# Four small fp32 transposing matmuls, moved along the TensorE queue from the first second product to the third quarter of the first w1

## Chip, cores and metric

The kernel runs on one core of a Trainium2 chip. The metric is the device time of one execution in microseconds, as a median of several runs; before the change it is 359.48 us (three runs, 359.46 to 359.53).

## What is computed

Attention over 4 batches and 8 heads, 768 tokens of 64 numbers, in which a token sees the 128 last tokens and 4 sink tokens; and behind it a mixture of four expert networks over the 3072 tokens, each token's experts weighted with its normalised probabilities.

```python
keep = is_sink | in_window                      # 4 sinks, window of 128
a = softmax(where(keep, q @ k.T / sqrt(D), -1e9))
x = (a @ v)                                     # heads side by side: [3072, 512]
p = domain_probs / (domain_probs.sum(-1, keepdims=True) + 1e-09)
for e in range(4):
    h = maximum(x @ w1[e], 0.0)                 # 512 -> 1024
    out += p[:, e:e + 1] * (h @ w2[e])          # 1024 -> 512
```

## The kernel before

**Tiling and stages.** Tokens are taken in groups of 256 (three groups g a batch b). For each group attention gives a transposed tile `xT` of bf16. For each expert e a *first product* makes H = relu(x w1): it is worked in four quarters j of 256 hidden columns, each 8 matmuls into one PSUM bank `hps` (L1114), after which ACT (L1127) or DVE (L1129) writes the quarter of H to SBUF. A *second product* multiplies H by w2 in 8 matmuls into one of two PSUM banks `acc[0]` and `acc[1]` (L1453), used in turn; ACT (L1465) or DVE (L1469 to L1471) then scales by the token's probability and adds to the output tile. Later groups take a form with seven products in place of eight for both (L1202, L1376); the change doesn't touch them.

**Who sets the order.** The program is written out by a planner in Python: the loop at the end of the kernel holds a clock for each engine (`t`), for each bank the time when it is free (`ring`, `acc_free`), and a list of tasks that other engines still have to run; at each turn it emits the candidate that is ready first. Every engine then works its own list strictly in the order in which the planner emitted it, and waits for semaphores where its data come from elsewhere. What matters here of the planner: `acc_free[i]` tells it when bank `acc[i]` may be written again, and a bank that counts as free may also be given to idle matmuls that it puts in where PE would stand still.

**The stretch of the change.** It lies in the first batch, some 18 to 24 us into the span. In the order of PE's list:

- the first product of the first group with expert 0: quarters 0 and 1 (L1114), with score matmuls (L738) and sink scores (L699) between them, then score matmuls, then quarter 2, the third
- the value products of attention (L798 and L805), which DVE normalises (reciprocal L832, product L835 into `onat`), and the transposes of the result (L864), which are copied to `xT` by DVE or ACT
- quarter 3 of expert 0 and four more transposes (L864)
- the four matmuls of `gates` (L966), and the first second product (L1453), into `acc[0]`

`gates` (L963 to L974) turns the probabilities: they are loaded as `dp`, 24 rows (blocks of 128 tokens) of 128 x 4 numbers, by one DMA of SP's queue (L478), issued right after the first q rows and ahead of the sinks (L546). One matmul for each expert, with a 24 x 24 fp32 identity, turns 24 x 128 into 128 x 24 in `acc[1]`. DVE sums over the experts (L968), adds a small number (L969), takes the reciprocal (L970) and multiplies (L971) into `scale_t`, which the scaling of all second products of the first batch reads. DVE also normalises the same probabilities by row for the later batches (L484 to L487); the two lists of instructions lie among each other on DVE.

w1 of expert 0 comes in four quarters by four DMAs of POOL's queue (L353), its w2 in two halves (L364), all issued early and landing one after the other; the first matmul of a quarter waits for that quarter's landing. `acc[1]` holds nothing else before its first second product: only the warming and idle matmuls of zeros (L533) write to it.

Of the kernel before, what the change touches and what calls it, by code (L numbers as in the profile page):

```python
# [16 lines left out]
def kernel(  # L17
# [17 lines left out]
    E, Dm, F = moe_w1.shape  # L35
# [71 lines left out]
    t = {"pe": 1200.0, "act": 0.0, "dve": 0.0, "pool": 1280.0, "sp": 800.0, "sw": 5900.0, "hw": 0.0}  # L107
    def by(x):

        return x[sum(t["pe"] > at for at in SPLIT)]  # L110
# [5 lines left out]
    def pe(cols, *deps, n=1, switch=0):  # L116
        t["pe"] = max([t["pe"], *deps])
        rate = 2.4 if t["pe"] > WARM else 1.2
        t["pe"] += cols / rate + 2.5 * n + 95 * switch
        return t["pe"] + 215  # L120
# [6 lines left out]
    def dve(cols, *deps, rate=0.96, fixed=157):  # L127
        at = max([t["dve"], *deps])
        t["dve"] = at + fixed - 85 + cols / rate
        return at + fixed + 35 + cols / rate  # L130
# [10 lines left out]
    def pick(part=True):  # L141

        return min(range(6), key=lambda i: (max(ring[i], t["pe"]), part == whole[i], ring[i]))

    def bank(i, shape, dtype, name, all_columns=False):

        whole[i] = all_columns
        return psum.tile(shape, dtype, name=name, tag=f"r{i}", bufs=1)

    def take(i, until):  # L150
        ring[i] = until
# [3 lines left out]
    def later(engine, ready, slack, run):  # L155

        pend.append((ready, ready + slack, engine, run))
# [35 lines left out]
    def clock(engine, cols, rate=0.96, fixed=157):  # L193
        return act(cols) if engine == "act" else dve(cols, rate=rate, fixed=fixed)
# [175 lines left out]
    def halves(e):  # L370
        return [slice(0, Dout)] if e else [slice(0, Dout // 2), slice(Dout // 2, Dout)]
# [99 lines left out]
    NT = Ntok // P  # L471
# [35 lines left out]
    def load_gates():  # L507

        while gates_at[0] < 1e11 and len(gate_sb) < len(mix.order) and (
            len(gate_sb) < NGATE or mix.order[len(gate_sb) - NGATE] in mix.finished  # L510
        ):
            b, g, e = mix.order[len(gate_sb)]
            load_gate(b * NG + g, e)
# [14 lines left out]
    acc = [psum.tile([P, 2 * G], FP32, name=f"acc{i}", tag=f"o{i}", bufs=1) for i in range(2)]  # L528
# [431 lines left out]

    scale_t = consts.tile([P, NT, E], FP32, name="scale_t")

    def gates():  # L963
        pt = acc[1][:, 0:E * NT].rearrange("p (e t) -> p e t", e=E)
        for e in range(E):
            nc.tensor.transpose(pt[:, e], dp[:, :, e], identf[0:NT, 0:NT])  # L966
        rs = consts.tile([P, NT], FP32, name="rs")
        nc.vector.reduce_sum(out=rs, in_=pt.rearrange("p e t -> p t e"), axis=AX.X)  # L968
        nc.vector.tensor_scalar_add(out=rs, in0=rs, scalar1=1e-9)  # L969
        nc.vector.reciprocal(out=rs, in_=rs)  # L970
        nc.vector.tensor_mul(  # L971
            scale_t, pt.rearrange("p e t -> p t e"), rs[:, :, None].to_broadcast([P, NT, E]),
        )
        acc_free[1] = dve(600, pe(400, acc_free[1]))  # L974

    PAIRS = [(b, g) for b in range(1, B) for g in range(NG)]
    CHAIN = ("P1", "P2", "P6", "P5", "P7", "P3", "P4")
    acc_free = [0.0, 0.0]
    out_sb = {}

    class Mixture:
# [96 lines left out]
        def emit_first(self, what, ready):  # L1078

            if what[0] == "early":  # L1080
                g = what[1]
                e = self.early[g].pop(0)
                u = self.opened(0, g, e)
                self.open.append(u)
                j = u["left"][0]
            elif what[0] == "unit":
                if not gate_sb:
                    load_gates()
                u = self.opened(*self.units.pop(0))
                self.open.append(u)  # L1090
                j = u["left"][0]
            else:
                u, j = what
            b, g, e = u["unit"]
            if j in (0, "P1") and (b, e) == (0, E - 1) and not gate_sb:
                load_gates()
            u["left"].remove(j)
            if not u["left"]:
                self.open.remove(u)
                left1[e] -= 1  # L1100
                if (b, g) not in PAIRS:
                    self.second += [(g, s, e, c) for c in halves(e) for s in range(2)]
            self.since += 1
            self.credit += (2 * QF * P if u["fast"] else 2 * NDB * G)
            if u["fast"]:
                self.emit_fast(u, j, ready)
                return
            slot = pick(False)
            h = bank(slot, [P, 2, G], FP32, "hps", True)
            ring[slot] = 1e12  # L1110
            for i in range(2):
                fb = 2 * j + i
                for db in range(NDB):
                    nc.tensor.matmul(  # L1114
                        h[:, i].rearrange("p (q n) -> p q n", q=2), lhsT=w1_sb[e][:, db, fb * P:(fb + 1) * P],
                        rhs=xT[b, g][:, :, db],
                        start=(i == 0 and db == 0), stop=(db == NDB - 1), skip_group_check=True,
                    )
            end = pe(2 * NDB * G, ready, n=2 * NDB)
            self.done += 2 * NDB * G  # L1120
            dst = self.H[b, g, e][:, j // 2, 2 * (j % 2):2 * (j % 2) + 2]
            dst = dst.rearrange("p f t n -> p f (t n)")
            part = self.H_part[b, g, e]
            if (b, g) not in PAIRS:
                def run(engine):
                    if engine == "act":
                        nc.scalar.activation(out=dst, in_=h, func=AF.Relu)  # L1127
                    else:
                        nc.vector.tensor_scalar(out=dst, in0=h, scalar1=0.0, scalar2=None, op0=ALU.max)  # L1129
                    at = clock(engine, 2 * G)  # L1130
                    take(slot, at)
                    part(at)
                later("any", end, 400, run)
                return
            gate = gate_sb[b * NG + g, e].rearrange("p t n -> p (t n)")[:, None, :].to_broadcast([P, 2, G])

            def run(engine):
                nc.vector.scalar_tensor_tensor(
                    out=dst, in0=h, scalar=0.0, in1=gate, op0=ALU.max, op1=ALU.mult,
                )  # L1140
                at = dve(2 * G, fixed=152)
                take(slot, at)
                part(at)
            later("dve", end, by(GATE0), run)
# [290 lines left out]
        def emit_second(self):  # L1435
# [5 lines left out]
            if g not in out_sb:  # L1441
                out_sb[g] = mo.tile([P, 2, Dout], FP32, name="osb0", tag=f"wide{g}" if g < 2 else "osb", bufs=1)
                if g == 0:
                    gates()
                    ready = max(ready, acc_free[self.turn % 2])
# [77 lines left out]
    while mix.more() or att.more():  # L1523
# [49 lines left out]
        s2, p = mix.second_ready(), mix.product_ready()  # L1573
# [67 lines left out]
```

## Time and profile before

| What | Value |
|---|---|
| median of the runs | 359.48 us (359.46 to 359.53) |
| the profiled execution: its time | 359.52 us |
| its span, first to last instruction | 357.8 us |
| granted TensorE clock | 1.000 |
| DVE, ACT, POOL busy | 296.2, 172.1, 69.0 us |
| the four matmuls L966 | first start 22.85 us, busy 0.65 us |

All durations in the text come from that one profiled execution, so they stand against its 359.52 us; the 1.7 us beside its span lie before the first and after the last instruction. A line such as `22.85 0.65 PE L966 MATMUL acc<-scratch 24*128 24x24 f32 x4` of the timeline is: start in us, length in us from the first start to the last end, engine, line of the kernel, operation, tiles written and read, shapes, how many; a bracket behind it tells how long the engine stood idle before it, and what ended that. PEld is the loading of weights, which overlaps with PE's matmuls. In the chain of waits a row is start, length, engine and line.

### The profile page before, as it was taken

The numbers are of one execution on the slowest core, as the hardware profiler recorded it, in microseconds if no ns is written. First come the engines' busy times: TensorE is split into PE (matmuls) and PEld (weight loads), VectorE is DVE, ScalarE is ACT, GpSimd is POOL, SyncE is SP. The second block draws the span as 40 slices with busy tenths as digits, with TensorE's granted clock in tenths as the row PEclk, the third lists the DMA queues.
The fourth block names the chain that finished last, engine by engine and source line by source line (L and its number), as shares of the span: only waits on it lengthen the run. The fifth ranks groups of instructions, "written<-read, shape, count | busy, mean of one in ns | idle before, by whom it ended". The sixth has DMA issues, their size and how long they took to land.

```text
span 357.8 us, 10767 instructions
## 1 busy us (share of the span) xinstructions
PE 350.9 (98%) x4525; PEld 302.6 (85%) x4534; DVE 296.2 (83%) x635; ACT 172.1 (48%) x440; POOL 69.0 (19%) x89
## 2 busy tenths in 40 slices
PE   8999999999999999999999999999999999999996
PEld 4688859757768698898998899899999999999985
DVE  5896689856978799899789889789899997898750
ACT  5958717458964555557455565554223203313110
POOL 8844117220942191010200000000000000000000
PEclk9999999999999999999999999999999999999999
DMA  9999999999999999168990211213111112000021
GB/s 174 185 190 204 210 207 176 184 156 179 131 144 169 191 146 165 49 63 151 141 124 22 54 44 50 60 62 60 31 45 62 31 31 76 16 29 33 0 75 45
DMA packets 115261, 37.26 MB, mean 104 GB/s; under 512 B 96533, under 2 KB 110709, under 8 KB 115213
## 3 DMA queue, kind: packets, MB, share of 16 engines
q0 software_dynamic: 75456, 17.31, 52.6%
q1 hardware_dynamic: 38700, 18.75, 26.2%
q8 instruction: 35, 0.57, 0.7%
q10 hardware_dynamic: 1056, 0.52, 0.6%
q14 instruction: 14, 0.11, 0.1%
HBM read 40.45 MB, written 9.49 MB: 140 GB/s over the span
## 4 chain that ended last, share of the span: by engine, by line
PE 94%; DVE 2%; DMA 2%; ACT 1%; issue 0%; ACTq 0%
PE cps L1202 34%; PE acc L1376 31%; PE acc L1453 12%; PE hps L1114 8%; PE sps L738 3%; PE od L805 3%; DMA raw<-in_k_dram 2%; DVE aT L773 1%; PE od L798 1%; DVE onat L835 1%; PE tx L864 0%; ACT aT L764 0%; PE sinks L699 0%; DVE H L1129 0%; PE tr L632 0%
## 5 line engine op out<-in xcount | busy, mean ns | idle before, releaser
L1202 PEld LDWEIGHTS <-w 128*128 128x128 bf16 x1248 | 76.8, 98 | 2.5 <-issue 0.6
L1376 PEld LDWEIGHTS <-H 128*128 128x128 bf16 x600 | 55.1, 98 | 7.3 <-issue 2.0
L764 ACT ACTIVATE aT<-sps 128x512 bf16<-128x512 f32 (+1 forms) x96 | 47.1, 575 | 24.6 <-PE sps L738 24.3
L1235 DVE SCALAR_TENSOR_TENSOR H<-cps,gates 128x512 bf16<-128x512 f32 x84 | 56.4, 681 | 1.5 <-PE cps L1202 0.7
L1376 PE MATMUL acc<-w,H 128*128 128x256 bf16 x360 | 49.4, 273 | 0.0
L1202 PEld LDWEIGHTS <-vf 128*128 128x128 bf16 x768 | 47.2, 98 | 1.6 <-issue 0.3
L1202 PE MATMUL cps<-T,w 128*128 128x128 bf16 x624 | 47.3, 219 | 0.0
L1202 PE MATMUL cps<-xT,w 128*128 128x128 bf16 x624 | 46.6, 219 | 0.0
L1453 PE MATMUL acc<-w,H 128*128 128x512 bf16 (+1 forms) x231 | 45.2, 335 | 0.5
L844 ACT ACTIVATE onat<-od,R 128x64 bf16<-128x64 f32 x144 | 33.0, 331 | 23.3 <-DVE R L832 23.2
L1248 ACT COPY cps<-cps 128x512 f32<-128x512 f32 x39 | 22.8, 584 | 41.8 <-PE cps L1202 35.2
L1202 PE MATMUL cps<-T,vf 128*128 128x128 bf16 x512 | 38.1, 219 | 0.0
L1114 PE MATMUL hps<-xT,w 128*128 128x256 bf16 x288 | 36.0, 273 | 0.9 <-DMA w<-in_moe_w_dram 0.9
L1453 PEld LDWEIGHTS <-H 128*128 128x128 bf16 x240 | 22.5, 98 | 14.3 <-issue 0.3
L340 POOL DMA_DIRECT2D vx<-in_v_dram x24 | 21.3, 895 | 59.9 <-PE od L805 47.4
L1114 PEld LDWEIGHTS <-w 128*128 128x128 bf16 x288 | 27.1, 98 | 5.1 <-DMA w<-in_moe_w_dram 1.5
L1376 PEld LDWEIGHTS <-S 128*128 128x128 bf16 x288 | 27.4, 98 | 3.3 <-issue 0.4
L1255 DVE TENSOR_TENSOR cps<-H,cps 128x512 f32<-128x512 f32 x33 | 22.8, 691 | 8.0 <-PE cps L1202 5.7
L1418 ACT COPY osb<-acc 128x256 f32<-128x256 f32 x28 | 10.5, 376 | 33.3 <-PE acc L1376 33.2
L1270 DVE TENSOR_TENSOR H<-H,cps 128x512 f32<-128x512 f32 x33 | 22.5, 682 | 3.9 <-PE cps L1202 3.8
L1261 ACT COPY H<-cps 128x512 f32<-128x512 f32 x33 | 19.7, 596 | 9.5 <-PE cps L1202 9.5
L1376 PE MATMUL acc<-wf,H 128*128 128x256 bf16 x176 | 23.7, 273 | 0.0
(130 smaller groups left out, 550.8 us busy)
## 6 DMA issues: line engine op xcount, KB each, us to landing
w<-in_moe_w_dram POOLq DMA_DIRECT2D x6, 1024.0 KB, 20.9
out_dram<-osb SPq DMA_DIRECT2D x19, 256.0 KB
gates<-gate_rows SPq DMA_DIRECT2D x36, 128.0 KB
vx<-in_v_dram POOLq DMA_DIRECT2D x24, 128.0 KB, 8.0
rows<-in_q_dram POOLq DMA_DIRECT2D x12, 128.0 KB, 5.8
rows<-in_k_dram POOLq DMA_DIRECT2D x12, 128.0 KB, 6.2
w<-in_moe_w_dram POOLq DMA_DIRECT2D x4, 256.0 KB, 9.2
w<-in_moe_w_dram POOLq DMA_DIRECT2D x2, 512.0 KB, 12.6
```

Of the source, the lines that this page charges most:

```text
L340: nc.gpsimd.dma_start(out=vx[tb][:, :, 0:D], in_=v[b, :, tb * P:(tb + 1) * P, :].rearrange("h p d -> p h d"),)
L764: nc.scalar.activation(out=a[:, ph], in_=sps[ph][:, 0:w], func=AF.Exp, scale=scale)
L844: nc.scalar.mul(o[:, qi, hp, ph * D:(ph + 1) * D], od[:, qi, ph, 0:D], R[:, qi, ph])
L1114: nc.tensor.matmul(h[:, i].rearrange("p (q n) -> p q n", q=2), lhsT=w1_sb[e][:, db, fb * P:(fb + 1) * P], rhs=xT[b, g][:, :, db], start=(i ...
L1202: nc.tensor.matmul(y[:, f], lhsT=A[:, d, f * P:(f + 1) * P], rhs=T[:, d], start=(m in ("P1", "P5") and f == 0 and d == 0), stop=(d == 1), ...
L1235: nc.vector.scalar_tensor_tensor(out=dst, in0=src, scalar=0.0, in1=gate, op0=ALU.max, op1=ALU.mult)
L1248: nc.scalar.copy(out=tiles["Y"], in_=y)
L1255: nc.vector.tensor_add(tiles["V"], c5, tiles["X"])
L1261: nc.scalar.copy(out=c5, in_=y)
L1270: nc.vector.tensor_add(c5, c5, y)
L1376: nc.tensor.matmul(x, lhsT=self.operand(b, g, e, m)[:, f], rhs=forms[e][m][:, f], start=(k == 0 and f == 0 and m in (("P1", "P5", "P2") if ...
L1453: nc.tensor.matmul(op, lhsT=H[:, fb // QF, fb % QF, s], rhs=w2_sb[e][:, fb, c], start=(fb == 0), stop=(fb == NFB - 1),)
```

## The change

The four matmuls get a function of their own, `gates_turned`, which also marks `acc[1]` as taken. It is called when the planner emits quarter 2 of the first product of expert 0, ahead of its eight matmuls. The DVE part stays in `gates`, where it was, and frees the bank as before.

```diff
-    def gates():
-        pt = acc[1][:, 0:E * NT].rearrange("p (e t) -> p e t", e=E)
+    pt = acc[1][:, 0:E * NT].rearrange("p (e t) -> p e t", e=E)
+
+    def gates_turned():
         for e in range(E):
             nc.tensor.transpose(pt[:, e], dp[:, :, e], identf[0:NT, 0:NT])
+        acc_free[1] = 1e12
+
+    def gates():
         rs = consts.tile([P, NT], FP32, name="rs")
...
-        acc_free[1] = dve(600, pe(400, acc_free[1]))
+        acc_free[1] = dve(600, pe(400))
...
             if u["fast"]:
                 self.emit_fast(u, j, ready)
                 return
+            if (e, j) == (0, 2) and acc_free[1] == 0.0:
+                gates_turned()
             slot = pick(False)
```

The planner's clocks are the same at every step: the 400 columns of the four matmuls are still charged where `gates` stands. The lists of ACT, POOL and SP are the same instruction by instruction, DVE's is the same but for one wait for PE that L968 no longer has, and on PE the four matmuls alone change their place. In the changed kernel the lines behind the edit are 6 higher (L1114 is L1120, L1453 is L1459), and L966 is L967.

## Prediction

> **What bounds the kernel now.** I read the page's head and the shares of its chain first, then the busy time by stretches, then what PE waits for.
>
> ```profile
> span 357.8 us, 10767 instructions
> PE 350.9 (98%) x4525; PEld 302.6 (85%) x4534; DVE 296.2 (83%) x635; ACT 172.1 (48%) x440; POOL 69.0 (19%) x89
> PE 94%; DVE 2%; DMA 2%; ACT 1%; issue 0%; ACTq 0%
> ```
>
> ```profile
> 15.00:21.00 6.00, 5.22 (x71) 3.84 (x72) 5.74 (x14) 4.75 (x10) 4.95 (x9) 1.00 1.46 197
> 18.20:18.78 0.58, 0.00 (x1) 0.00 (x1) 0.58 (x3) 0.52 (x2) 0.12 (x1) 1.00 1.45 198
> 23.44:354.20 330.76, 330.28 (x4294) 288.45 (x4302) 277.71 (x566) 155.72 (x402) 50.88 (x60) 1.00 0.76 99
> ```
>
> PE is busy nearly all the time, and 94% of the chain that ended last is PE's. In the stretches the columns are: beginning and end, its length, then busy us of PE, PEld, DVE, ACT, POOL, the granted clock, DMA, GB/s. From 23.44 us to the end PE is busy for 330.28 of 330.76 us at a granted clock of 1.00: what makes PE arrive there earlier moves the end, unless another engine then comes late. From 15 to 21 us it is otherwise: DVE has 5.74 of 6.00, PE 5.22, and PE does nothing from 18.20 to 18.78. The chain of waits has the change of hands:
>
> ```profile
> 17.77 1.00 DVE aT L773 x3
> ...
> 19.38 1.00 DVE aT L773 x3
> ...
> 20.94 0.05 issue
> 20.99 0.28 PE tx L864 x2
> ...
> 22.92 0.58 PE acc L966 x4
> ```
>
> Up to 20.94 the chain runs on DVE, and PE's work there is not on it; from 20.99 it is PE. The four matmuls (L966) stand on the PE part, with 0.58 us. PE's list of waits has one row for the hole at 18.20:
>
> ```profile
> PE hps L1114 <- DMA w<-in_moe_w_dram: 0.9, 2, 0.6
> ```
>
> Its longest, 0.6, is this hole: it ends when the third quarter of the first w1 lands. In the rows below, x4 with 0.65 is a group of four, and the row with x1 is the last of them by itself.
>
> **The change part by part.** No instruction is added or lost, and none on ACT, POOL or SP (so no DMA and no queue of theirs) changes its place. On PE the four L966 matmuls go from ahead of the first L1453 product to ahead of the third quarter's first L1114 weight load. They carry their wait for the probabilities' load with them. On DVE the L968 reduction keeps its place and loses its wait for PE.
>
> **Removed at 22.85.** PE's timeline there:
>
> ```profile
> 21.54 0.29 PE L864 MATMUL tx<-ident,onat 128*128 128x128 bf16 x2
> 21.66 1.04 PE L1114 MATMUL hps<-xT,w 128*128 128x256 bf16 x8
> 22.53 0.39 PE L864 MATMUL tx<-ident,onat 128*128 128x128 bf16 x4
> 22.85 0.65 PE L966 MATMUL acc<-scratch 24*128 24x24 f32 x4
> 23.23 0.27 PE L966 MATMUL acc<-scratch 24*128 24x24 f32 x1
> 23.44 1.05 PE L1453 MATMUL acc<-w,H 128*128 128x256 bf16 x8
> ```
>
> I go by starts. Two transposes and the step to the next bf16 matmul take 21.66 - 21.54 = 0.12, 0.06 each. Four from 22.53 thus (4 x 0.057 before rounding) let L1453 start at 22.53 + 0.23 = 22.76 where it now starts at 23.44: 0.68 us. No row shows a direct step from L864 to L1453. The last L864 starts at 22.53 + 3 x 0.057 = 22.70. If the step cost as much as the one to L966 (22.85 - 22.70 = 0.15), L1453 would start at 22.85 and the gain be 0.59; if nothing, at 22.70, 0.74. I take 0.68, since the row with the same kind of follower (a bf16 weight load of 128 columns) is L1114, and keep 0.59 and 0.74.
>
> The chain prints 0.58 for the same four. [...]
>
> **What is late next.** Two things could hold L1453 at 22.76. Its last two weight loads read what ACT writes at 22.73; and its first matmul needs the first half of w2 (the 512 KB issue at 10.44):
>
> ```profile
> 22.73 0.60 ACT L1127 ACTIVATE H<-hps 128x512 bf16<-128x512 f32 x1 [0.50 <-PE hps L1114]
> 24.00 0.10 PEld L1453 LDWEIGHTS <-H 128*128 128x128 bf16 x1
> w<-in_moe_w_dram POOLq DMA_DIRECT2D x1, 512.0 KB, 12.0
> 23.07 0.76 POOL L353 DMA_DIRECT2D w<-in_moe_w_dram  x1 [2.12 <-DMA w<-in_moe_w_dram]
> ```
>
> ACT ends at 23.33; a start follows about 0.05 later (20.94 to 20.99 in the chain). The seventh load, now at 24.00, would be due at 23.32 and can start at 23.38: 0.06 late. A weight load normally runs 0.1 ahead of its matmul, so some of that is hidden; I charge half, 0.03. w2 lands at 10.44 + 12.0 = 22.44, ahead of 22.76. So **-0.65 us**.
>
> DVE doesn't follow, and needn't:
>
> ```profile
> 23.48 0.37 DVE L485 TENSOR_SCALAR scratch<-scratch 24x128 f32<-24x128 f32 x1
> 23.61 0.24 DVE L968 TENSOR_REDUCE rs<-acc 128x24 f32<-128x96 f32 x1
> 24.46 0.26 DVE L971 TENSOR_TENSOR scale_t<-acc,rs 128x96 f32<-128x96 f32 x1
> 26.07 1.04 PE L1453 MATMUL acc<-w,H 128*128 128x256 bf16 x8
> ```
>
> L968 stands right behind L485, so its lost wait gives nothing, and scale_t stays at 24.72. The next product overwrites the bank that L971 reads; it comes at 26.07 - 0.68 = 25.39, still 0.6 after.
>
> **Added at 18.2.**
>
> ```profile
> 17.99 0.21 PE L738 MATMUL sps<-qkT 64*128 64x128 bf16 x1
> 18.78 1.05 PE L1114 MATMUL hps<-xT,w 128*128 128x256 bf16 x8 [0.58 <-DMA w<-in_moe_w_dram]
> 19.90 0.29 PE L805 MATMUL od<-vx,aT 128*128 128x65 bf16 x4
> 20.30 0.17 DVE L832 RECIPROCAL R<-od 128x4 f32<-128x4 f32 x1
> ```
>
> The last score matmul starts at 17.99. With the steps of the old place (0.15 to the first, 23.23 - 22.85 = 0.38 among the four, 23.44 - 23.23 = 0.21 to the next) the quarter could start at 18.73, and its weights are there at 18.78 only. The cost is zero, and the cover is that transfer. The bounds: zero, since PE before 20.94 is not on the chain and so can't give anything back, and the full 0.74 of these steps if nothing hid. Should the block run over, or the quarter land early, there is a second cover: the first value products end at 19.90 + 0.29 = 20.19 and DVE takes them up at 20.30, after its masks, so 0.1 us of lateness is free; what goes beyond it counts one for one.
>
> **Sum**: 0.00 - 0.68 + 0.03 = -0.65. The profiled execution took 359.52 us around its span of 357.8; it becomes 358.87. The median of the runs is 359.48, so **358.83**, with 358.77 to 358.92 from the two ends of the step alone (0.71 and 0.56 after the same 0.03).
>
> **Later stretches.** The one place after 23.44 that a transfer feeds closely is the regrouping of the last q and k rows:
>
> ```profile
> 28.26 0.88 POOL L257 DMA_DIRECT2D qkn<-in_q_dram  x1 [0.68 <-DMA runs<-in_k_dram]
> 29.26 1.31 ACT L296 COPY qkn<-runs 128x256 bf16<-128x256 bf16 x4
> 30.86 1.29 DVE L296 COPY qkT<-tr 128x512 bf16<-128x512 bf16 x2 [0.41 <-PE tr L632]
> 32.30 0.62 PE L738 MATMUL sps<-qkT 64*128 64x128 bf16 x12
> ```
>
> The rows are there by 28.26, ACT starts on them at 29.26 behind work that PE feeds: 1.0 us of room for 0.68. DVE's copies wait for PE (0.41), so they move up with it, although PE's L738 comes only 0.15 after their end.
>
> **Rivals.**
> 1. *The next wait takes the place of the one removed.* POOL waited for the same half of w2 until 23.07, 0.6 behind that landing. If PE got the word only then, L1453 starts at 23.07 and the gain is 0.37: 359.11. Against it: the landing in the view of the DMA issues is 22.44.
> 2. *Given back later.* If the copies at 30.86 didn't move, only 32.30 - 32.15 - 0.05 = 0.10 would be left: 359.38. For it: DVE is busy for 84% after 23.44 (277.71 of 330.76), and its turn can come late. Against it: both its copies and ACT's wait for PE.
> 3. *Slower: the block waits.* PE works in order, so if the probabilities are late, the third quarter and all behind it stand still. Their first reader now is at 22.49, long after:
>
> ```profile
> 1.86 0.51 SPq L478 DMA_DIRECT2D scratch<-in_moe_domain_probs_dram  x1
> 15.50 1.05 POOL L677 TENSOR_TENSOR vsd<-vsf,sel 128x520 bf16<-128x520 f32 x1
> 22.49 0.66 DVE L484 TENSOR_REDUCE scratch<-scratch 24x128 f32<-24x512 f32 x1
> ```
>
> A landing as late as that would start the quarter at 22.49 + 0.38 + 0.21 = 23.08, 4.30 late; less 0.10 of cover and the 0.68 won, +3.5: 363.0. It decides from 18.78 + 0.10 + 0.68 = 19.56 on. Against it: the load is issued at 1.86, and the sinks, loaded behind it on the same queue, are read at 15.50.
>
> **How the numbers follow.** 0.2% of 359.48 is 0.72 us, about what a measurement can tell from no change; the forecast of -0.65 stays just inside it. Forecast 0.68, rival 1 0.15, rival 2 0.10, rival 3 0.07. The step's upper end (0.74) and the scatter of the runs (359.46 to 359.53) put about a third of the forecast's chance beyond 0.72: faster 0.22, within 0.71, slower 0.07. The range goes from 358.65, the upper end with that scatter, to 359.25, which takes in rival 1 and half of the way to rival 2.
>
> **What would show it.** Right: the four (L967 in the changed kernel) on PE between about 18.1 and 18.7 with the third quarter still at 18.78; onat's turn still at 20.99; the first second product (now L1459) at 22.76 and everything on PE after it 0.65 earlier; scale_t unchanged at 24.72. Wrong: L1459 held by ACT or by w2 past 22.85; the quarter's start after 18.9; a new idle time of PE, or an advance on PE at 40 us that is smaller than at 23 us.

## The result and the profile after

The changed kernel takes 358.77 us (median of 11 runs, 358.69 to 358.93) against 359.53 us (11 runs, 359.39 to 359.99) of the kernel before on the same chip: 0.76 us less, a ratio of 0.9978 with a 95% interval of 0.9969 to 0.9988. So it is faster, by an amount whose middle (0.22%) lies just past the 0.2% that the forecast took as the bound; the interval has that bound within it. The profiled execution took 358.69 us, with a span of 357.0 against 357.8.

The page's head, its busy times and the shares of its chain after:

```profile
span 357.0 us, 10767 instructions
PE 351.1 (98%) x4525; PEld 303.1 (85%) x4534; DVE 296.2 (83%) x635; ACT 172.1 (48%) x440; POOL 68.9 (19%) x89
PE 95%; DMA 2%; POOL 2%; issue 0%; ACT 0%; DVE 0%
```

The same instructions and, within 0.5 us, the same busy times as before. The time was not taken out of any engine's work, it was idle time of PE. The busy time by stretches, in the columns of the prediction, shows where:

```profile
15.00:21.00 6.00, 5.82 (x77) 4.49 (x78) 5.74 (x14) 4.64 (x10) 4.82 (x8) 1.00 1.45 197
22.61:353.40 330.79, 330.31 (x4296) 288.40 (x4302) 278.55 (x568) 156.25 (x403) 50.99 (x60) 1.00 0.76 99
```

From 15 to 21 us PE is now busy for 5.82 instead of 5.22 us, about the hole of 0.58 us at 18.20 more. The last row begins at the first second product, as the one of before did, and is the same stretch: before it had 0.48 us of idle PE in 330.76, now it has 0.48 in 330.79. PE's list of waits has lost its 0.6 and keeps only the wait of the first quarter:

```profile
PE hps L1120 <- DMA w<-in_moe_w_dram: 0.4, 1, 0.4
```

PE's timeline around the change:

```profile
17.99 0.66 PE L967 MATMUL acc<-scratch 24*128 24x24 f32 x4
18.69 1.05 PE L1120 MATMUL hps<-xT,w 128*128 128x256 bf16 x8
...
20.85 0.28 PE L864 MATMUL tx<-ident,onat 128*128 128x128 bf16 x2
...
22.39 0.39 PE L864 MATMUL tx<-ident,onat 128*128 128x128 bf16 x4
22.61 1.04 PE L1459 MATMUL acc<-w,H 128*128 128x256 bf16 x8
```

The four stand at 17.99, and the third quarter starts at 18.69. No bracket shows idle time ahead of it, but a bracket counts from the shown end of the matmul before. By starts a short wait is left. The last of the four by itself, and the landing of the third quarter in the view of the DMA issues (issued at 8.91):

```profile
18.37 0.27 PE L967 MATMUL acc<-scratch 24*128 24x24 f32 x1
w<-in_moe_w_dram POOLq DMA_DIRECT2D x1, 256.0 KB, 9.7
```

From the last of the four to the next product were 0.21 us at the old place (23.23 to 23.44). So the quarter could have started at 18.58. Its weights land at about 8.91 + 9.7 = 18.61, and it starts at 18.69: the wait for the landing is shorter, but it is still there.

From onat's turn (the first transposes of `onat`, L864) to the first second product were 23.44 - 20.99 = 2.45 us; now they are 22.61 - 20.85 = 1.76. So 0.69 went there by these rounded rows (0.68 by the unrounded starts). The other 0.14 of the 0.83 lies ahead of onat's turn, and ahead of the four too. DVE, on which onat's turn waits, before and after:

```profile
17.09 0.68 DVE L1129 TENSOR_SCALAR H<-hps 128x512 bf16<-128x512 f32 x1
16.95 0.68 DVE L1135 TENSOR_SCALAR H<-hps 128x512 bf16<-128x512 f32 x1
```

DVE has the 0.14 already at 16.95, where both kernels have worked the same instructions. So this part is a difference between the two executions and not the change.

The chain that ended last, between 16.9 and 23.7 us:

```profile
18.06 0.59 PE acc L967 x4
18.64 0.04 issue
18.69 1.05 PE hps L1120 x8
...
20.85 0.28 PE tx L864 x2
...
22.55 0.22 PE tx L864 x4
22.78 0.87 PE acc L1459 x8
```

This view has to be read with care. DVE is gone from it, and the four matmuls are on it with 0.59 us, where they had 0.58 before. A reader could take from this that nothing was won, or that 0.59 more is to be had by leaving them out. But the chain decides by shown ends. The four are shown to end at 18.06 + 0.59 = 18.65, just behind the landing, so the chain goes on to them, although by starts the quarter waited for the landing. At onat's turn it is the same: the value products are shown to end at 20.80, DVE's `onat` (L835) at 20.36 + 0.42 = 20.78, so the chain takes the value products. The weight load of the transposes has its true releaser:

```profile
20.84 0.11 PEld L864 LDWEIGHTS <-onat 128*128 128x128 bf16 x2 [0.16 <-DVE onat L835]
```

So the third quarter still waits for its landing and onat's turn still for DVE, as before the change, and the four hold neither. The first experiment tests that.

### The profile page after: what moved, and what is told of

Its sections match the earlier page's. It is cut to its first block, busy times and chain, and to the rows that moved or that the text cites. A ratio compares the mean times of both kernels' runs of the same rounds, so it can differ in the third digit from the quotient of the medians.

```text
span 357.0 us, 10767 instructions
## 1 busy us (share of the span) xinstructions
PE 351.1 (98%) x4525; PEld 303.1 (85%) x4534; DVE 296.2 (83%) x635; ACT 172.1 (48%) x440; POOL 68.9 (19%) x89
## 4 chain that ended last, share of the span: by engine, by line
PE 95%; DMA 2%; POOL 2%; issue 0%; ACT 0%; DVE 0%
PE cps L1208 34%; PE acc L1382 31%; PE acc L1459 12%; PE hps L1120 9%; PE sps L738 3%; PE od L805 3%; DMA w<-in_moe_w_dram 2%; POOL vx L340 1%; PE od L798 1%; POOL runs L317 0%; PE sinks L699 0%; PE tx L864 0%; PE tr L632 0%; POOL scratch L553 0%; PE acc L967 0%
## 5 line engine op out<-in xcount | busy, mean ns | idle before, releaser
L1459 PE MATMUL acc<-w,H 128*128 128x512 bf16 (+1 forms) x231 | 45.2, 335 | 0.5
L1120 PE MATMUL hps<-xT,w 128*128 128x256 bf16 x288 | 36.0, 273 | 0.4 <-DMA w<-in_moe_w_dram 0.4
L1459 PEld LDWEIGHTS <-H 128*128 128x128 bf16 x240 | 22.5, 98 | 14.3 <-issue 0.5
L1120 PEld LDWEIGHTS <-w 128*128 128x128 bf16 x288 | 27.0, 98 | 4.6 <-DMA w<-in_moe_w_dram 0.8
L1382 PE MATMUL acc<-wf,H 128*128 128x256 bf16 x176 | 23.7, 273 | 0.0
```

The costliest lines, as they stand in the source:

```text
L1120: nc.tensor.matmul(h[:, i].rearrange("p (q n) -> p q n", q=2), lhsT=w1_sb[e][:, db, fb * P:(fb + 1) * P], rhs=xT[b, g][:, :, db], start=(i ...
L1382: nc.tensor.matmul(x, lhsT=self.operand(b, g, e, m)[:, f], rhs=forms[e][m][:, f], start=(k == 0 and f == 0 and m in (("P1", "P5", "P2") if ...
L1459: nc.tensor.matmul(op, lhsT=H[:, fb // QF, fb % QF, s], rhs=w2_sb[e][:, fb, c], start=(fb == 0), stop=(fb == NFB - 1),)
```

## The experiments

Theory A is the forecast's: at the old place the four stand between transposes and a second product on an engine that hardly waits from there to the end, and cost 0.68 us; at the new place they run while PE would wait for the third quarter of w1, and cost nothing up to that landing and about 0.1 us beyond. Against it could stand that the gain has another source than the place (the rivals in the expectations of the first four runs), that the new place has a price which something else hides, or that only a place in front of just this wait is free. All edits are to the changed kernel, and each time is compared with the kernel before on the same chip.

**The four left out.** This kernel computes no probabilities: DVE's part of `gates` reads a bank that the four haven't written.

```diff
     def gates_turned():
-        for e in range(E):
-            nc.tensor.transpose(pt[:, e], dp[:, :, e], identf[0:NT, 0:NT])
         acc_free[1] = 1e12
```

> The four transposing matmuls are left out altogether, so the gates of the first batch are not computed from the probabilities (the DVE steps read zeros). Theory A (the four stood on PE's own path and now lie wholly inside the wait for the third quarter of w1): leaving them out gives no more than moving them did, 0.70 to 0.80 us under before, and quarter 2 still starts at its landing. Rival B (they still cost something at the new place): up to 0.58 more, 1.0 to 1.3 us under before.

358.78 us (358.61 to 358.88) against 359.48, ratio 0.998 (0.9971 to 0.9988): no faster than the changed kernel. In its PE timeline the hole is back, with its releaser:

```profile
18.66 1.05 PE L1118 MATMUL hps<-xT,w 128*128 128x256 bf16 x8 [0.55 <-DMA w<-in_moe_w_dram]
20.90 0.29 PE L864 MATMUL tx<-ident,onat 128*128 128x128 bf16 x2
22.66 1.04 PE L1457 MATMUL acc<-w,H 128*128 128x256 bf16 x8
```

The quarter starts at 18.66 without the four and at 18.69 with them. At the new place they cost nothing that can be measured, as theory A has it and against rival B, and the 0.59 on the chain is no gain still to be had.

**The four at both places.** They are emitted at the new place and again at the head of `gates`.

```diff
     def gates():
+        for e in range(E):
+            nc.tensor.transpose(pt[:, e], dp[:, :, e], identf[0:NT, 0:NT])
         rs = consts.tile([P, NT], FP32, name="rs")
```

> The four at the new place and once more at the old one. Theory A: the old place alone costs, so the time of before, 0.0 to 0.1 us under it, with 0.68 us between the last transpose of attention and the second product. Rival C (what counted was that the sums start early, or that the run began earlier by chance): 0.3 us under before or more.

359.54 us (359.48 to 359.91) against 359.48, ratio 1.0002 (0.9993 to 1.0011).

```profile
22.84 0.65 PE L972 MATMUL acc<-scratch 24*128 24x24 f32 x4
23.42 0.83 PE L1461 MATMUL acc<-w,H 128*128 128x256 bf16 x6
```

The whole gain is gone; the second copy stands at 22.84, where the four stood before (22.85), and the second product is back at 23.42. So it is the block's absence at the old place that gives the time, and nothing else of the edit does.

**One quarter later.** The block goes in front of the fourth quarter, which waits for no transfer (in the rows of before it stands at 21.66, with no wait shown ahead of it).

```diff
-            if (e, j) == (0, 2) and acc_free[1] == 0.0:
+            if (e, j) == (0, 3) and acc_free[1] == 0.0:
```

> The four in front of quarter 3, one quarter later, where PE does not wait for a landing (its weights landed 1.8 us before). Theory A: 0.00 to 0.10 us under before, since PE is the bound from 20.9 us on. Rival C (any place well ahead of the second product does): 0.6 to 0.8 us under before.

359.50 us (359.39 to 359.79) against 359.48, ratio 1.0001 (0.9992 to 1.001).

```profile
18.84 1.05 PE L1120 MATMUL hps<-xT,w 128*128 128x256 bf16 x8 [0.67 <-DMA w<-in_moe_w_dram]
...
21.75 0.66 PE L967 MATMUL acc<-scratch 24*128 24x24 f32 x4
...
23.44 0.82 PE L1459 MATMUL acc<-w,H 128*128 128x256 bf16 x6
```

Moved by a microsecond along PE's list, but behind onat's turn, the block costs what it cost. It isn't the neighbour (a first instead of a second product) that decides, but whether PE waits there.

**Each of the four twice, at the new place.**

```diff
-        for e in range(E):
+        for e in 2 * list(range(E)):
```

> Eight in place of four at the new place (each twice, the second time over the first). They take 0.15 + 7 x 0.127 + 0.21 = 1.25 us from the last score matmul on, the wait there gives 0.79. Theory A: the quarter starts 0.45 late, of which 0.10 is free behind DVE: 0.35 to 0.45 us slower than four there, so 0.3 to 0.4 us under before. Rival D (DVE alone covers this stretch, and PE has much more than 0.10 free): as fast as four, 0.7 us under before.

359.13 us (359.01 to 359.26) against 359.48, ratio 0.9989 (0.9981 to 0.9998): 0.35 under before, A's number and not D's, and 0.35 slower than the kernel with the four left out.

```profile
18.08 1.13 PE L967 MATMUL acc<-scratch 24*128 24x24 f32 x8
19.15 1.05 PE L1120 MATMUL hps<-xT,w 128*128 128x256 bf16 x8
...
20.59 0.18 DVE L832 RECIPROCAL R<-od 128x4 f32<-128x4 f32 x1 [0.27 <-PE od L805]
```

Here the cover is seen to run out. The quarter starts at 19.15, 0.37 later than before the change (18.78). DVE's reciprocal, which waited for nothing at 20.30, now waits 0.27 for the value products and starts 0.29 later. So 0.37 - 0.29 = 0.08 was covered, where the forecast put 0.10; two executions differ by as much (onat's turn is at 20.99 before and at 20.90 with the four left out), so this says no more than that the cover is small.

**One of the four stays.** Expert 0's matmul goes back to `gates`, three move.

```diff
     def gates_turned():
-        for e in range(E):
+        for e in range(1, E):
...
     def gates():
+        nc.tensor.transpose(pt[:, 0], dp[:, :, 0], identf[0:NT, 0:NT])
```

> One of the four (expert 0's) stays at the old place, three go to the third quarter. By the starts of before the step into a fp32 matmul takes 0.15 us, the one out of it 0.21, and a plain step 0.06, so one alone costs 0.15 + 0.21 - 0.06 = 0.30 of the 0.68. Theory A1 (most of the block's price for a single one is going in and out): 0.38 to 0.42 us under before. Theory A2 (the price is a quarter for each): 0.51 to 0.55 under before.

359.15 us (359.01 to 359.74) against 359.56, ratio 0.999 (0.9981 to 0.9998): a gain of 0.41 of the 0.7.

```profile
22.50 0.39 PE L864 MATMUL tx<-ident,onat 128*128 128x128 bf16 x4
22.82 0.29 PE L971 MATMUL acc<-scratch 24*128 24x24 f32 x1
23.04 1.05 PE L1460 MATMUL acc<-w,H 128*128 128x256 bf16 x8
```

One small matmul makes the second product start 23.04 - 22.50 = 0.54 behind the first L864, where it is 22.61 - 22.39 = 0.22 without: 0.32 for the first, 0.12 to 0.13 for each further one. Three quarters of the moved work give little more than half of the gain, since going from bf16 to this block and back costs about 0.2 by itself. For the whole gain the whole block had to move.

**In front of the second and of the first quarter.**

```diff
-            if (e, j) == (0, 2) and acc_free[1] == 0.0:
+            if (e, j) == (0, 1) and acc_free[1] == 0.0:
```

> The four in front of quarter 1, where PE waits for next to nothing. Theory A (lateness on PE before 18.7 us is taken up by the wait for the third quarter, as long as DVE gets the scores in time; the quarter and the scores behind it come 0.59 late, and DVE reaches them only at about 19.6 to 20.0): 0.6 to 0.75 us under before, like the third quarter. Rival E (the hole has to be where the four stand): the 0.59 is paid, 0.1 to 0.2 us under before.

358.85 us (358.76 to 359.27) against 359.56, ratio 0.998 (0.9972 to 0.9989): -0.71.

```profile
16.59 0.66 PE L967 MATMUL acc<-scratch 24*128 24x24 f32 x4
17.18 1.05 PE L1120 MATMUL hps<-xT,w 128*128 128x256 bf16 x8
18.77 1.05 PE L1120 MATMUL hps<-xT,w 128*128 128x256 bf16 x8 [0.23 <-DMA w<-in_moe_w_dram]
```

The second quarter has no wait for a transfer in its row, but it comes 0.54 later (17.18 against 16.64) and the hole behind it shrinks to 0.23: PE reaches the landing early all the same. So the block needn't stand at the wait itself, as long as the work between can be late. That speaks against E, by which the lateness would have been paid.

```diff
+            if (e, j) == (0, 0) and acc_free[1] == 0.0:
```

> The four in front of quarter 0, in the 0.34 us wait for its landing at 15.1. The quarter starts 0.18 late. Theory A: that is taken up by the waits for the quarters behind it: 0.65 to 0.75 us under before. Rival E: 0.5 to 0.55 us under before.

358.81 us (358.68 to 359.04) against 359.56, ratio 0.9979 (0.997 to 0.9988): -0.75, the same once more, now in front of the first quarter, which itself waits for a landing. That quarter starts at 15.32 instead of 15.11, but the third waits 0.57 for its landing again, and by then the lateness is gone. The probabilities are there by then too.

**Each four times.** This was to stretch the cost line of the doubled block to sixteen.

```diff
-        for e in range(E):
+        for e in 4 * list(range(E)):
```

> Sixteen at the new place (each four times over). 0.15 + 15 x 0.127 + 0.21 = 2.26 us from the last score matmul, against 0.79 of wait and 0.10 behind DVE. Theory A: 1.02 us over the eight, 0.65 to 0.75 us slower than before. Rival D (still covered in part by DVE): 0.3 us slower than before or less.

A miss: 360.91 us (360.01 to 361.34, 6 runs) against 359.56, ratio 1.0033 (1.0021 to 1.0045). The median hides two groups. Three executions took 361.28, 361.28 and 361.34 at a mean granted clock of 0.994; the others 360.01, 360.14 and 360.53 at 0.998 to 1.000, which is 0.45 to 0.97 over before and nearer to A's 0.65 to 0.75 than to D's 0.3 or less. The profile is of the first group. The busy time by stretches (the granted clock is the third column from the right) and PE's timeline:

```profile
17.95:20.56 2.61, 2.61 (x25) 2.51 (x23) 2.25 (x6) 1.37 (x4) 1.57 (x3) 1.00 1.46 197
20.56:23.97 3.41, 3.41 (x47) 3.22 (x45) 1.77 (x6) 0.97 (x2) 1.02 (x2) 0.50 1.52 195
```

```profile
17.95 2.09 PE L967 MATMUL acc<-scratch 24*128 24x24 f32 x16
19.98 1.38 PE L1120 MATMUL hps<-xT,w 128*128 128x256 bf16 x8
...
21.27 0.42 PE L805 MATMUL od<-vx,aT 128*128 128x65 bf16 x4
```

For 3.41 us the granted clock is half (ahead of it and behind it 1.00), the value products take 0.42 instead of 0.28, and the quarter 1.38 instead of 1.05. The cost line itself holds: 17.95 to 19.98 are 2.03 us for sixteen, 18.08 to 19.15 were 1.07 for eight, 0.12 each. What failed is the tacit assumption that PE's clock stays at 1.00.

**The same time in bf16.** Is it the delay, or what fills it? 27 bf16 matmuls of zeros into the other bank stand ahead of the four.

```diff
     def gates_turned():
+        for _ in range(27):
+            nc.tensor.matmul(acc[0][:, 0:P], lhsT=zeros[:, 0:P], rhs=zeros[:, 0:P], start=True, stop=True)
         for e in range(E):
```

> The four at the new place, and ahead of them 27 bf16 matmuls of 128 columns of zeros into the other bank (27 x 0.056 = 1.51 us), about as long as the twelve more small fp32 matmuls of the run with sixteen. [...] Rival G (any delay of the stretch by 1.3 us lets the clock fall): 361.0 to 361.4 us in half of the runs or more.

360.26 us (360.14 to 360.39, 11 runs) against 359.49, ratio 1.002 (1.0011 to 1.0029).

```profile
18.10 1.68 PE L967 MATMUL acc<-zeros 128*128 128x128 bf16 x27
19.71 0.65 PE L969 MATMUL acc<-scratch 24*128 24x24 f32 x4
20.30 1.05 PE L1122 MATMUL hps<-xT,w 128*128 128x256 bf16 x8
```

```profile
20.00:22.00 2.00, 2.00 (x35) 1.87 (x35) 0.57 (x4) 0.60 (x1) 0.76 (x1) 1.00 1.45 197
```

The quarter is later still (20.30 against 19.98), but the clock stays at 1.00, in every one of the 11 executions (means 0.998 to 1.000). So a delay of this length didn't lower it here, and G falls. What the sixteen have and this kernel hasn't is the long run of small fp32 matmuls; why such a run should lower the clock isn't shown by this. The sixteen ran on another chip than this kernel, and only six times; the kernel before, on the sixteen's chip, was at 0.998 or more in all its 29 executions. The loss, 0.77, is above the upper end of the 0.4 to 0.7 that the author expected of an unchanged clock, since the 27 take 19.71 - 18.10 = 1.61 us, 0.06 each: the second product comes at 24.21, 0.77 behind the 23.44 of before.

**Each three times.**

```diff
-        for e in range(E):
+        for e in 3 * list(range(E)):
```

> Twelve at the new place (each three times over): 0.15 + 11 x 0.127 + 0.21 = 1.76 us. At an unchanged clock 0.4 to 0.5 us over the run with eight, so 0.05 to 0.15 us over before. [...]

359.70 us (359.54 to 360.24, 11 runs) against 359.49, ratio 1.0006 (0.9997 to 1.0015), at 0.998 or more of the clock in all 11. That is 0.21 over before where 0.05 to 0.15 was expected, and 0.57 over eight where 0.4 to 0.5 was. In the profiles the quarter is 0.61 later than with eight (19.76 against 19.15): 0.48 of this are the four more matmuls (1.55 against 1.07 from the block's start to the quarter's, 0.12 each), and 0.13 because the block itself starts later (18.21 against 18.08).

**All runs side by side.** The start of the first second product in each profile, against the 23.44 of before, and the time against the kernel before on the same chip:

| Kernel | second product starts | against 23.44 | time against before |
|---|---|---|---|
| changed kernel | 22.61 | -0.83 | -0.76 |
| four left out | 22.66 | -0.78 | -0.70 |
| first quarter | 22.71 | -0.73 | -0.75 |
| second quarter | 22.70 | -0.74 | -0.71 |
| one stays | 23.04 | -0.40 | -0.41 |
| eight | 23.06 | -0.38 | -0.35 |
| both places | 23.42 | -0.02 | +0.06 |
| fourth quarter | 23.44 | 0.00 | +0.02 |
| twelve | 23.67 | +0.23 | +0.21 |
| bf16 filler | 24.21 | +0.77 | +0.77 |
| sixteen, its profiled execution | 25.20 | +1.76 | +1.72 |

Over a range of 2.6 us the time follows this one start, to 0.08. No kernel's median is lower than the changed kernel's: with the block's cost at zero, there is nothing more in its place.

## Why the prediction was right

The forecast was 358.83, the result 358.77, and the mechanism is the one that it gave. By its steps:

- *The block's cost at the old place, 0.68.* Measured as 0.68 from onat's turn to the second product (2.45 to 1.76 in the rounded rows), and restored by putting the four back. The step with no row of its own, from L864 straight to a second product, was taken from the row with the same kind of follower; it is 22.61 - 22.39 = 0.22 for four, where 0.23 was assumed. In each of the seven profiles at a full clock that have nothing of the block between these two, they are 1.76 or 1.77 apart; in the three that have all of it, 2.44 to 2.46. The chain's 0.58 would have been the wrong number: the sum by starts was met, the one by ends missed by 0.1. To go by starts was the author's choice; the rows of before already show that the ends mislead, since the four are busy for 0.65 us there, while from L966's first start to L1453's start are 0.59.
- *0.03 for the seventh weight load.* This is the term that was mis-sized: it cost nothing. The rows after, of ACT and of the weight loads from 23.2 us on:

```profile
22.59 0.60 ACT L1133 ACTIVATE H<-hps 128x512 bf16<-128x512 f32 x1 [0.50 <-PE hps L1120]
```

```profile
23.24 0.13 PEld L1459 LDWEIGHTS <-H 128*128 128x128 bf16 x2
```

  ACT ends at 23.19 and the seventh load starts at 23.24: the 0.05 behind ACT is there, and so is the small delay, since the last two loads now take 0.13 together. But the weight load's lead swallows it whole: from L1459 to the product after it PE needs 23.49 - 22.61 = 0.88 us, before it was 24.32 - 23.44 = 0.88.
- *Nothing to pay at 18.2.* Right, and shown by leaving the four out: without them the quarter started at 18.66, with them at 18.69. By its steps it could have started at 18.58, so about 0.1 us was to spare, where the forecast had 0.05 (18.73 against 18.78). The block began at 17.99 and not at 17.99 + 0.15 = 18.14; in the other kernels that have such a block there it began between 17.95 and 18.21, so the margin differs from one execution to the next. So does the landing: the quarter that waits for it started at 18.78 before the change and at 18.84 in the kernel with the block in front of the fourth quarter. The second cover, behind DVE's masks, was put at 0.10; the doubled block gave 0.08.
- *Onat's turn still at 20.99.* It stands at 20.85. In the other profiles without a lengthened block it is 20.90 (four left out), 20.94, 20.94, 20.96, 20.98 and 20.98. The kernel with the four left out has the same lists as the one before up to 22.85 and is 0.09 earlier, and in the changed kernel DVE has its lead of 0.14 before the four begin. So this is the difference between two executions, and it makes the profiled pair differ by 0.83 where the medians differ by 0.76. Without the 0.03 the forecast would have been -0.68; the four kernels that have the block off the path show -0.70 to -0.76. The 0.02 to 0.08 beyond are not explained. The median of the kernel before was 359.48 to 359.56 in its four sets of runs, so they are about as large as what the comparison leaves uncertain.
- *DVE gets nothing from its lost wait.* Right:

```profile
23.34 0.42 DVE L485 TENSOR_SCALAR scratch<-scratch 24x128 f32<-24x128 f32 x1
23.47 0.29 DVE L972 TENSOR_REDUCE rs<-acc 128x24 f32<-128x96 f32 x1
24.35 0.26 DVE L975 TENSOR_TENSOR scale_t<-acc,rs 128x96 f32<-128x96 f32 x1
```

  L972 is 0.14 earlier, exactly as its neighbour L485 is, and scale_t is done at 24.61 instead of 24.72.
- *The later stretches carry it.* DVE's two copies moved from 30.86 to 30.02 with the wait for PE ahead of them as long as before, and ACT's last copy, the end of the chain, starts at 353.55 instead of 354.36:

```profile
30.02 1.29 DVE L296 COPY qkT<-tr 128x512 bf16<-128x512 bf16 x2 [0.41 <-PE tr L632]
...
353.55 0.37 ACT L1424 COPY osb<-acc 128x256 f32<-128x256 f32 x1 [4.87 <-PE acc L1382]
```

  Of the 0.83 at the second product, 0.81 arrive there.

The rivals: the *next wait* falls, since L1459 runs at 22.61, before POOL gets its word of w2's half at 22.98, so PE doesn't wait for what POOL waits for. The half, issued at 10.38, lands 11.9 later, at 22.28, 0.33 ahead of L1459; a second product more than about 0.3 earlier would have to wait for it:

```profile
22.98 0.76 POOL L353 DMA_DIRECT2D w<-in_moe_w_dram  x1 [2.12 <-DMA w<-in_moe_w_dram]
w<-in_moe_w_dram POOLq DMA_DIRECT2D x1, 512.0 KB, 11.9
```

*Given back later* falls with the last copy. *The block waits for the probabilities* falls too: it started right behind the score matmuls, and in front of the first quarter it cost nothing either. The chances put 0.71 on a change within 0.2%: the forecast lay 0.07 us inside that bound and the result 0.04 us beyond it, and what carried it over are the 0.03 that wasn't paid and the open remainder.

## What to carry to other kernels

Here one engine hardly waited from one point to the end (0.48 us in 330.76), and a small block behind that point cost its full time, 0.68 us; ahead of it, in front of a wait of 0.58 us for a transfer, it cost nothing that could be measured (the quarter started at 18.69 with it, at 18.66 without). So look in the timeline of the bound engine for the idle time that a DMA ends, and move such blocks ahead of it as far as they fit, and whole: going into and out of this block had a price of its own, about 0.2 us. Work out what leaving the path is worth from the starts of matmuls (0.68, which was met), not from the chain's lengths (0.58), and ask what lies right beside the chain before counting a step on it as a gain still to be had: here a landing and another engine, hidden by shown ends. Size the block to the hole: here four matmuls, 0.59 us by their starts, were free in front of the landing, and four more, 0.48 us, cost 0.35.

## What the runs showed of the hardware

- **A long run of small fp32 matmuls was followed by half the clock of TensorE, while PE was shown busy.** Sixteen of them in 2.03 us were followed by 3.41 us at a granted clock of 0.50 in the profiled execution, and three of six executions, at a mean granted clock of 0.994, took 1.3 us more than the fastest, at 1.000. The sixteen ran on one chip only. Four, eight (1.07 us) and twelve (1.55 us) never showed it in 11 executions each, at means of 0.998 or more, nor did 1.61 us of bf16 matmuls with four small ones behind. PE is shown busy for 2.61 of the 2.61 us ahead of the fall, though a busy time rests on the shown ends. Why the clock fell, and why in some executions only, isn't shown: the transposing, the fp32 and the 24 rows and columns were not tried apart.
- **Going into and out of a block of small fp32 matmuls cost more than one of them.** The first between bf16 ones added 0.32 us and each further one 0.12 to 0.13, so about 0.2 go to the change itself; a step between bf16 matmuls of 128 columns is 0.06. Whether the type or the 24 rows and columns make this price was not tried apart.
